# Four of six gate chunks of the last batch by Strassen's scheme, with sums formed a batch or two ahead

## The chip, the cores and the metric

The kernel runs on one core of a Trainium2 chip (trn2). The metric is device time in microseconds (us) from one launch, lower is better. The core has TensorE (PE: matrix products into the eight banks of PSUM), VectorE (DVE), ScalarE (ACT) and GpSimd (POOL) for element-wise work, and SyncE (SP), whose queue issues nearly all DMA transfers of this kernel. Each engine works through its own list of instructions in order and waits on semaphores for the others.

## The reference

```python
# q, k, v: 4 batches x 8 heads x 576 tokens x 64; everything float32
attn = softmax(q @ k.T / 8 + min(bias, 0), causal)      # bias from a running sum of max(s, 0)
x = concat_heads(attn @ v)                              # 2304 x 512
x = (silu(x @ w_gate) * (x @ w_val)) @ w_out            # 512 -> 1536 -> 512, "layer 1"
x = silu(x @ w_in2) @ w_out2                            # 512 -> 2048 -> 512, "layer 2"
```

## The kernel before

Every float32 product is made of three: each operand is split into a rounded high part and a low rest, and `mm3` issues high x high, high x low and low x high into one PSUM bank. Layer 1 runs batch by batch (0 to 3), each batch in nine chunks (`L1`): six "gv" chunks (gate and value columns for 256 of the 1536 hidden units) and three "o1" chunks (product with `w_out`). I number the chunks through: 0 to 35, batch 3 is 27 to 35. A gv chunk has four steps (`gate`: 2 groups of 128 hidden units x 2 halves of 288 tokens); a step has 24 matmuls of 128 x 128 by 128 x 288 for the gate, in one bank, and for the value, in a second, so a chunk has 96. ACT applies Silu (batch 3; Tanh before) to the gate's bank, DVE multiplies it with the value's bank (L534), ACT rounds the product to `h` high (L112), GpSimd subtracts for `h` low (L536). The pool `ps_m` has four banks, so the step after next takes the banks again: gate bank free after Silu, value bank free after L534. In batches 0 to 2 attention for the next batch is woven between the steps.

Weights of a chunk come as two 1 MB halves from DRAM (`w_half`, L396), where batch 0 has put them split into high and low; the pool has room for two chunks, so a chunk's load is issued when the chunk before the previous one is done. Beside layer 1 runs the preparation of layer 2's weights: raw pieces are loaded (`ahead_load`), decoded by ACT and DVE (`ahead`, L409 to L415), summed by GpSimd (`u_sum`, L473), cut by ACT and GpSimd (`u_cut`, L481) and stored (`u_store`, L486). Layer 2 already uses Strassen's scheme (`up2`, `down2`): seven products of sums of quarter blocks in place of eight.

What sets the order: PE's order is written by hand everywhere. Until the end of batch 2 a scheduler orders the other engines; in batch 3 and after all engines work in the order of the code.

Of the kernel before, what the change touches and what calls it, by code (L numbers as in the profile page):

```python
# [66 lines left out]
def kernel(  # L67
# [751 lines left out]
    def body():  # L819
# [101 lines left out]
        g = nc.gpsimd
        for c in range(last, n1):
            cur = chunk_steps(c)
            k = c - last
            more = [[] for _ in range(4)]
            extra = []
            if c + 1 < n1:
                more[0] += [lambda e=e: w_half(c + 1, e) for e in range(2)]
            i = tail_pieces.get(c)
            if i is not None:  # L930
                more[1].append(lambda i=i: ahead(i))
                if i % 2:
                    more[1].append(lambda q=i // 2: u_sum(q))
                    for e in range(2):
# [133 lines left out]
```

## Time and profile before

| what | value |
|---|---|
| device time of three runs | 1004.8, 1007.87, 1009.32 us; median 1007.87 us |
| the profiled execution's own time | 1005.74 us |
| its span, first to last instruction | 1004.0 us |
| PE, DVE, ACT, GpSimd busy | 99%, 56%, 52%, 59% of the span |
| granted TensorE clock | 1.00 after the first fortieth of the span |
| first and last matmul of batch 3 start at | 531.17 and 646.07 us |

The spans below are of the profiled execution. A busy share says how long an engine had any instruction in flight; whether it bounds the kernel is read from who waited for whom.

### The profile page before, as it was taken

The numbers are of one execution on the slowest core, as the hardware profiler recorded it, in microseconds if no ns is written. First come the engines' busy times: TensorE is split into PE (matmuls) and PEld (weight loads), VectorE is DVE, ScalarE is ACT, GpSimd is POOL, SyncE is SP. The second block draws the span as 40 slices with busy tenths as digits, with TensorE's granted clock in tenths as the row PEclk, the third lists the DMA queues.
The fourth block names the chain that finished last, engine by engine and source line by source line (L and its number), as shares of the span: only waits on it lengthen the run. The fifth ranks groups of instructions, "written<-read, shape, count | busy, mean of one in ns | idle before, by whom it ended". The sixth has DMA issues, their size and how long they took to land.

```text
span 1004.0 us, 19497 instructions
## 1 busy us (share of the span) xinstructions
PE 990.0 (99%) x6924; PEld 929.5 (93%) x6924; DVE 557.9 (56%) x1408; ACT 522.8 (52%) x1267; POOL 592.6 (59%) x748
## 2 busy tenths in 40 slices
PE   8999999999999999999999999999999999999998
PEld 6588889999998899899899999999999999999998
DVE  6868576635546544535542323366666667665555
ACT  6779788525666435656533543244544335543333
POOL 5967747515876555747541665356567458674445
PEclk8999999999999999999999999999999999999999
DMA  8898779667788799766768776797867866896662
GB/s 222 213 329 301 263 272 307 216 222 247 279 295 273 254 309 307 278 235 234 261 242 298 268 293 249 271 379 285 293 238 279 320 219 247 298 342 234 246 224 101
DMA packets 81618, 267.17 MB, mean 266 GB/s; under 512 B 9904, under 2 KB 29360, under 8 KB 66160
## 3 DMA queue, kind: packets, MB, share of 16 engines
q1 hardware_dynamic: 81376, 265.73, 75.7%
q8 instruction: 54, 0.88, 0.3%
q14 instruction: 44, 0.36, 0.1%
q10 hardware_dynamic: 144, 0.20, 0.1%
HBM read 208.15 MB, written 57.75 MB: 265 GB/s over the span
## 4 chain that ended last, share of the span: by engine, by line
PE 89%; ACT 4%; DMA 3%; DVE 2%; issue 1%; POOL 1%; SPq 0%; POOLq 0%; DVEq 0%; ACTq 0%
PE pgv L522 9%; PE pgv L523 9%; PE pgv L524 9%; PE po L709 6%; PE po L710 6%; PE po L711 6%; PE pu L664 6%; PE pu L667 6%; PE pu L668 6%; PE po L522 5%; PE po L523 5%; PE po L524 5%; PE pv L351 5%; PE psc L218 4%; PE ptr L302 3%; ACT e L255 2%
## 5 line engine op out<-in xcount | busy, mean ns | idle before, releaser
L522 PE MATMUL pgv<-xt,wt 128*128 128x288 f32 x768 | 229.7, 299 | 2.1 <-DVE u L533 1.7
L523 PE MATMUL pgv<-xt,wt 128*128 128x288 f32 x768 | 226.2, 294 | 0.0
L524 PE MATMUL pgv<-xt,wt 128*128 128x288 f32 x768 | 226.1, 294 | 0.0
L641 POOL TENSOR_TENSOR h<-u,h 128x384 fp32r<-128x384 f32 x72 | 75.1, 1044 | 142.5 <-ACT h L112 134.9
L522 PEld LDWEIGHTS pgv<-xt,wt 128*128 128x128 f32 x768 | 144.1, 188 | 13.7 <-DVE m L235 6.3
L523 PEld LDWEIGHTS pgv<-xt,wt 128*128 128x128 f32 x768 | 144.1, 188 | 0.0
L524 PEld LDWEIGHTS pgv<-xt,wt 128*128 128x128 f32 x768 | 144.0, 188 | 0.0
L536 POOL TENSOR_TENSOR h<-u,h 128x288 fp32r<-128x288 f32 x96 | 78.9, 824 | 87.3 <-ACT h L112 85.0
L112 ACT ACTIVATE h<-u 128x288 fp32r<-128x288 f32 (+1 forms) x168 | 79.8, 475 | 97.0 <-DVE u L534 95.9
L522 PE MATMUL po<-h,wt 128*128 128x288 f32 x384 | 114.8, 299 | 0.0
L523 PE MATMUL po<-h,wt 128*128 128x288 f32 x384 | 113.1, 294 | 0.0
L524 PE MATMUL po<-h,wt 128*128 128x288 f32 x384 | 113.0, 294 | 0.0
L709 PE MATMUL po<-h,wt 128*128 128x384 f32 x336 | 112.4, 335 | 0.0
L710 PE MATMUL po<-h,wt 128*128 128x384 f32 x336 | 112.3, 334 | 0.0
L711 PE MATMUL po<-h,wt 128*128 128x384 f32 x336 | 112.3, 334 | 0.0
L664 PE MATMUL pu<-x,wt 128*128 128x384 f32 x330 | 111.8, 339 | 0.3 <-DMA wt<-wu_d 0.3
L668 PE MATMUL pu<-x,wt 128*128 128x384 f32 x330 | 111.7, 339 | 0.0
L667 PE MATMUL pu<-x,wt 128*128 128x384 f32 x330 | 111.7, 339 | 0.0
L641 POOL TENSOR_TENSOR h<-t,h 128x384 fp32r<-128x384 f32 x96 | 106.7, 1133 | 5.5 <-ACT h L112 5.5
L255 ACT ACTIVATE e<-e,m 64x64 f32<-64x64 f32 (+4 forms) x160 | 88.2, 553 | 30.7 <-DVE m L235 29.9
L670 ACT ACTIVATE s<-pu 128x384 f32<-128x384 f32 x48 | 23.6, 492 | 150.2 <-PE pu L668 150.2
L720 DVE TENSOR_TENSOR acc<-po,acc 128x384 f32<-128x384 f32 x144 | 76.8, 558 | 36.3 <-PE po L711 35.6
(115 smaller groups left out, 2187.4 us busy)
## 6 DMA issues: line engine op xcount, KB each, us to landing
wt<-w_d SPq DMA_DIRECT2D x54, 1024.0 KB, 7.0
wt<-wu_d SPq DMA_DIRECT2D x48, 1024.0 KB, 9.2
wt<-wu_d SPq DMA_DIRECT2D x47, 768.0 KB, 6.6
r<-in_w_dram SPq DMA_DIRECT2D x36, 512.0 KB, 6.5
w_d<-wt SPq DMA_DIRECT2D x18, 1024.0 KB, 8.4
r<-in_w_dram SPq DMA_DIRECT2D x64, 256.0 KB, 7.3
qkr<-in_qk_dram SPq DMA_DIRECT2D x32, 288.0 KB, 9.0
cumb<-cum_d SPq DMA_DIRECT2D x15, 576.0 KB, 9.7
```

The costliest lines, as they stand in the source:

```text
L112: act_last[:] = [nc.scalar.activation(out=out, in_=in_, func=AF.Copy, scale=scale).ins]
L255: nc.scalar.activation(out=e[:r, hd, :wd], in_=e[:r, hd, :wd], func=AF.Exp, bias=m[hd][:r], scale=-1.0, accum_out=put[hd],)
L522: nc.tensor.matmul(out=ps[:, :n], lhsT=a, rhs=xh, start=(k == 0), stop=False)
L523: nc.tensor.matmul(out=ps[:, :n], lhsT=a, rhs=xl, start=False, stop=False)
L524: nc.tensor.matmul(out=ps[:, :n], lhsT=c, rhs=xh, start=False, stop=(k == last))
L641: nc.gpsimd.tensor_tensor(out=h[:, 1], in0=u, in1=h[:, 0].bitcast(F32), op=ALU.subtract)
L664: nc.tensor.matmul(out=o, lhsT=a, rhs=x[:, 0, kk], start=fresh and kk == 0, stop=False, skip_group_check=True)
L667: nc.tensor.matmul(out=o, lhsT=a, rhs=x[:, 1, kk], stop=False, **more)
L668: nc.tensor.matmul(out=o, lhsT=c, rhs=x[:, 0, kk], stop=kk == 1, **more)
L709: nc.tensor.matmul(out=ps, lhsT=a, rhs=h[:, 0], start=fresh, stop=False, skip_group_check=True)
L710: nc.tensor.matmul(out=ps, lhsT=a, rhs=h[:, 1], stop=False, **more)
L711: nc.tensor.matmul(out=ps, lhsT=c, rhs=h[:, 0], stop=e == 1, **more)
```

## The change

In batch 3 the gv chunks at places 1, 2, 4 and 5 of the nine (chunks 28, 29, 31 and 32) use Strassen's scheme on 2 x 2 blocks (input halves x token halves). `quad` computes the gate (e = 0) and then the value (e = 1), each in seven products of six matmuls of 288 columns: 42 for each, 84 in a chunk. The four quarter results of the gate lie in the four banks of `ps_m`, those of the value in four banks of `ps_o`. Adding up the products takes, for each e, two ACT copies (`s0`, `s1`) and four DVE additions (`w`, and three more), of which two (into bank c and from it into `s1`) stand between the fourth product and the seventh, which adds to bank c.

Four sums of weight blocks for each of these chunks are formed by DVE from the split weights while these are in SBUF for batch 1 (gate half) and batch 2 (value half) (`s_make`, one addition 512 wide and four 128 wide, 16 times), stored to DRAM (16 transfers of 256 KB) and loaded again in batch 3 (`z_load`, 8 of 512 KB), where ACT rounds (`s_high`) and DVE subtracts (`s_low`, 1024 wide, both inputs in SBUF). The sums of the tokens are formed by DVE in two halves, the first in chunk 26, the second at the start of chunk 27 (`t_sum`, `t_cut`). The side work of batch 3 gets new places (a table of steps); `x2_load` moves from chunk 27 to chunk 30. Tanh writes straight into `u`, and the pool for `u` has three buffers in place of two.

```diff
+QUAD = (1, 2, 4, 5)
+MAKE = {
+    (1, 1): (2, 3), (1, 2): (0, 3), (1, 4): (1, 3), (1, 5): (0, 3),
+    (2, 1): (0, 2), (2, 2): (1, 3), (2, 4): (0, 2), (2, 5): (1, 3),
+}
...
-            th = tmp.tile([P, HB], F32, tag="th", name="th")[:, :n]
-            nc.scalar.activation(out=th, in_=pg[:, :n], func=AF.Tanh, scale=0.5)
+            nc.scalar.activation(out=u, in_=pg[:, :n], func=AF.Tanh, scale=0.5)
...
+    def t_sum(i, kk):
...
+            v.tensor_tensor(out=t, in0=a[:, 0], in1=b[:, 0], op=ALU.subtract)
+            v.tensor_tensor(out=d, in0=a[:, 1], in1=b[:, 1], op=ALU.subtract)
+            v.tensor_tensor(out=t, in0=t, in1=d, op=ALU.add)
+            return
...
+        v.tensor_tensor(out=t, in0=a[:, 0], in1=t, op=ALU.subtract)
+        v.tensor_tensor(out=t, in0=t, in1=a[:, 1], op=ALU.add)
+
+    def t_cut(i, kk, eng):
...
+        copy("a", x[:, 0], t)
+        eng.tensor_tensor(out=x[:, 1], in0=t, in1=x[:, 0].bitcast(F32), op=ALU.subtract)
+
+    def s_make(c, e, kk):
...
+        nc.vector.tensor_tensor(out=zs, in0=hi, in1=lo, op=ALU.add)
...
+            nc.vector.tensor_tensor(out=o, in0=a, in1=b, op=op)
+        nc.sync.dma_start(out=z_d[QUAD.index(place[stream[c]]), e, kk], in_=z)
...
+    def s_high(k, e):
+        qd["s", k, e] = qd["sp"].tile([P, 2, CW // 2], F32R, tag="sq", name="sq")
+        copy("a", qd["s", k, e][:, 0], qd["z", k, e])
+
+    def s_low(k, e):
+        s = qd["s", k, e]
+        nc.vector.tensor_tensor(out=s[:, 1], in0=qd["z", k, e], in1=s[:, 0].bitcast(F32), op=ALU.subtract)
+
+    def quad(c, i, e, pos):
...
+        if xi in (0, 1):
+            nc.scalar.activation(out=part(f"s{xi}"), in_=o, func=AF.Copy)
+        if xi == 3:
+            v.tensor_tensor(out=part("w"), in0=o, in1=qd["s0"], op=ALU.add)
+        if xi in (4, 5):
+            v.tensor_tensor(out=o, in0=o, in1=qd["w"], op=ALU.add)
+        if xi == 4:
+            v.tensor_tensor(out=qd["s1"], in0=o, in1=qd["s1"], op=ALU.add)
+            close(3, qd["s1"])
+        if xi in (2, 5, 6):
+            close({2: 0, 5: 1, 6: 2}[xi], o)
...
+        for i, at in ((1, -1), (4, -1), (3, -1), (6, 0)):
+            at_step(0, at, t_sum, i, 1)
+            at_step(0, at, t_cut, i, 1, v)
```

On DVE, at the start of chunk 27, this stood before (u is the product with the value's bank, dk and z32 decode a piece for layer 2):

```order
L565 SCALAR_TENSOR_TENSOR acc3_6384<-po_7679,acc3_6384 128x288
L534 TENSOR_TENSOR u_7742<-pgv_7729,u_7742 128x288
L534 TENSOR_TENSOR u_7777<-pgv_7764,u_7777 128x288
L412 SCALAR_TENSOR_TENSOR dk_7783<-z32_7782,dk_7783 128x512
L415 SCALAR_TENSOR_TENSOR z32_7782<-r64_7646,dk_7783 128x512
L534 TENSOR_TENSOR u_7818<-pgv_7805,u_7818 128x288
L534 TENSOR_TENSOR u_7853<-pgv_7840,u_7853 128x288
```

And this stands there now, from chunk 27's second gate product to the first additions of chunk 28 (tq and xq: token sums; sq: weight sums, zq as loaded; pq: banks of the scheme):

```order
L606 TENSOR_TENSOR xq_7611<-tq_7795,xq_7611 128x288
L540 TENSOR_TENSOR u_7879<-pgv_7866,u_7879 128x288
L633 TENSOR_TENSOR sq_7884<-zq_7791,sq_7884 128x1024
L540 TENSOR_TENSOR u_7916<-pgv_7903,u_7916 128x288
L633 TENSOR_TENSOR sq_7921<-zq_7793,sq_7921 128x1024
L419 SCALAR_TENSOR_TENSOR dk_7927<-z32_7926,dk_7927 128x512
L422 SCALAR_TENSOR_TENSOR z32_7926<-r64_7713,dk_7927 128x512
L540 TENSOR_TENSOR u_7961<-pgv_7948,u_7961 128x288
L683 TENSOR_TENSOR w_7990<-pq_7983,s0_7975 128x288
L633 TENSOR_TENSOR sq_7981<-zq_7887,sq_7981 128x1024
L685 TENSOR_TENSOR pq_8007<-pq_8007,w_7990 128x288
L687 TENSOR_TENSOR s1_8002<-pq_8007,s1_8002 128x288
```

Two weight sums and the decode now stand before the fourth product, and a third weight sum before the additions into bank c. Ahead of these rows, between acc3 and the second product, DVE has eight more rows of token sums.

On ACT, in the same stretch (u: Silu; h: high part; xq and sq: high parts of the sums), before:

```order
L529 ACTIVATE u_7742<-pgv_7716 128x288
L112 ACTIVATE h_7715<-u_7742 128x288
L529 ACTIVATE u_7777<-pgv_7751 128x288
L112 ACTIVATE h_7715<-u_7777 128x288
L409 ACTIVATE z32_7782<-r64_7646 128x512
L410 ACTIVATE dk_7783<-r64_7646 128x512
L529 ACTIVATE u_7818<-pgv_7792 128x288
L112 ACTIVATE h_7791<-u_7818 128x288
L529 ACTIVATE u_7853<-pgv_7827 128x288
```

And now, from the second Silu on:

```order
L536 ACTIVATE u_7879<-pgv_7853 128x288
L118 ACTIVATE h_7813<-u_7879 128x288
L118 ACTIVATE sq_7884<-zq_7791 128x1024
L536 ACTIVATE u_7916<-pgv_7890 128x288
L118 ACTIVATE h_7889<-u_7916 128x288
L118 ACTIVATE sq_7921<-zq_7793 128x1024
L416 ACTIVATE z32_7926<-r64_7713 128x512
L417 ACTIVATE dk_7927<-r64_7713 128x512
L536 ACTIVATE u_7961<-pgv_7935 128x288
L118 ACTIVATE h_7889<-u_7961 128x288
L681 ACTIVATE s0_7975<-pq_7968 128x288
L118 ACTIVATE sq_7981<-zq_7887 128x1024
```

The fourth Silu stands behind two weight sums and the decode, and the first copy of chunk 28 (`s0`) behind that.

On DVE, in chunk 21 (batch 2), ten rows of `s_make` (zm, two sums at once, for chunk 22) now stand around the last minimum of the scores (L242, two rows, L235 before) and ahead of the reciprocal that followed right behind it. The first six of the twelve rows there:

```order
L614 TENSOR_TENSOR zm_6633<-wt_6279 128x512
L614 TENSOR_TENSOR zm_6739<-wt_6279 128x512
L242 ISA e_6288,m_6332<-psc_6296,e_6288,m_6330 128x64
L242 ISA m_6332 128x1
L620 TENSOR_TENSOR zm_6633<-zm_6633 128x128
L620 TENSOR_TENSOR zm_6739<-zm_6739 128x128
```

The minimum, the reciprocal and what follows them now come after one pair of 512-wide additions, and the reciprocal after eight 128-wide ones too.

## Rows read from the trace of the kernel before

**Rows 1.** The page: busy time of the engines; the chain that ended last.
```profile
PE 990.0 (99%) x6924; PEld 929.5 (93%) x6924; DVE 557.9 (56%) x1408; ACT 522.8 (52%) x1267; POOL 592.6 (59%) x748
...
PE 89%; ACT 4%; DMA 3%; DVE 2%; issue 1%; POOL 1%; SPq 0%; POOLq 0%; DVEq 0%; ACTq 0%
```
**Rows 2.** Windows of batches 1, 2, 3: stretch, length, busy us by engine, clock, DMA.
```profile
220.65:375.87 155.22, 155.22 (x1206) 141.68 (x1205) 80.53 (x253) 86.74 (x233) 98.78 (x148) 1.00 0.82 280
375.87:531.17 155.30, 154.17 (x1195) 140.93 (x1193) 75.72 (x247) 86.24 (x232) 90.26 (x137) 1.00 0.74 255
531.17:646.40 115.23, 114.90 (x868) 114.70 (x867) 33.19 (x60) 44.67 (x88) 61.57 (x55) 1.00 0.76 279
```
**Rows 3.** Timeline of PE: first matmul of chunks 27 and 28, last of batch 3.
```profile
531.17 0.29 PE L522 MATMUL pgv<-xt,wt 128*128 128x288 f32 x1
...
543.89 0.29 PE L522 MATMUL pgv<-xt,wt 128*128 128x288 f32 x1
...
646.07 0.30 PE L524 MATMUL po<-h,wt 128*128 128x288 f32 x1
```
**Rows 4.** Timelines of PE and SP at batch 3's one gap (chunk 32).
```profile
596.22 0.29 PE L524 MATMUL pgv<-xt,wt 128*128 128x288 f32 x1
596.84 0.37 PE L522 MATMUL pgv<-xt,wt 128*128 128x288 f32 x1 [0.33 <-DMA wt<-w_d]
...
586.93 0.93 SPq L396 DMA_DIRECT2D wt<-w_d  x2
```
**Rows 5.** ACT and DVE in batch 3, by form: busy us, mean ns, idle before.
```profile
L112 ACT ACTIVATE h<-u 128x288 fp32r<-128x288 f32 x24 | 10.7, 445 | 34.6 <-DVE u L534 34.6
L529 ACT ACTIVATE u<-pgv 128x288 f32<-128x288 f32 x24 | 9.6, 402 | 17.1 <-PE pgv L524 14.5 <-POOL h L536 2.6
L112 ACT ACTIVATE cut<-s 128x1024 fp32r<-128x1024 f32 x4 | 4.2, 1044 | 0.0
...
L534 DVE TENSOR_TENSOR u<-pgv,u 128x288 f32<-128x288 f32 x24 | 10.9, 456 | 49.5 <-PE pgv L524 43.6 <-ACT u L529 4.1 <-POOL x L597 1.7
```
**Rows 6.** DVE with both inputs in SBUF, alone and beside GpSimd.
```profile
L618 DVE TENSOR_TENSOR stage<-x2r 128x384 f32<-128x384 f32 x4 | 2.2, 548 | 0.0
...
599.14 0.95 DVE L618 TENSOR_TENSOR tt<-x2r,tt 128x768 f32<-128x768 f32 x1
...
560.41 1.83 DVE L618 TENSOR_TENSOR tt<-x2r,tt 128x768 f32<-128x768 f32 x1
...
559.58 1.85 POOL L597 TENSOR_TENSOR x<-x2r,x 128x768 fp32r<-128x768 f32 x1
```
**Rows 7.** Timeline of DVE at chunk 27: last addition of chunk 26, fourth product.
```profile
531.37 0.46 DVE L565 SCALAR_TENSOR_TENSOR acc<-po,acc 128x288 f32<-128x288 f32 x1 [1.14 <-PE po L524]
...
544.16 0.46 DVE L534 TENSOR_TENSOR u<-pgv,u 128x288 f32<-128x288 f32 x1 [2.44 <-PE pgv L524]
```
**Rows 8.** Timeline of ACT in chunk 27: table, first Silu, decode, fourth Silu.
```profile
532.99 1.28 ACT L529 ACT_TABLE_LOAD   x1 [4.63 <-PE pgv L524]
534.28 0.41 ACT L529 ACTIVATE u<-pgv 128x288 f32<-128x288 f32 x1
...
538.67 0.66 ACT L409 ACTIVATE z<-r 128x512 f32<-128x512 f32 x1
...
542.55 0.41 ACT L529 ACTIVATE u<-pgv 128x288 f32<-128x288 f32 x1 [0.35 <-PE pgv L524]
```
**Rows 9.** DMA of `w_half` in batch 3, 16 issues.
```profile
DMA to landing us min/median/max: 5.4/7.6/10.0
```
**Rows 10.** Timeline of DVE in chunk 21: idle before its last wait.
```profile
442.76 0.22 DVE L235 CUSTOM_DVE_ANT_0 e<-psc,e 64x64 f32<-64x64 f32 x1 [6.78 <-PE psc L218]
```
**Rows 11.** Timelines of ACT and PE at the two gaps of batch 2.
```profile
400.02 1.06 ACT L112 ACTIVATE cut<-s 128x1024 fp32r<-128x1024 f32 x1 [3.99 <-DMA wu_d<-cut]
...
401.98 0.40 PE L522 MATMUL pgv<-xt,wt 128*128 128x288 f32 x1 [0.40 <-DVE u L533]
...
414.01 0.49 PE L351 MATMUL pv<-pt,vz 128*64 128x320 f32 x2 [0.74 <-DVE u L533]
```

More of the change, by code (lines that the diff above doesn't have):

```diff
@@ L92 @@
     dec_p = pool("dec", 2, scope=first_layer)
-    tmp_p = pool("tmp", 2, scope=first_layer)
+    tmp_p = pool("tmp", 3, scope=first_layer)
     h_p = pool("h", 6, scope=first_layer)
@@ L125 @@
     x2_d = dram.tile([KD, P, NT], F32, name="x2_d")
+    z_d = dram.tile([len(QUAD), 2, 2, P, DW], F32, name="z_d")
     w64 = w.bitcast(U32).rearrange("c p (n t) -> c p n t", t=2)
@@ L575, in chunk_steps @@
         kind, i = stream[c]
+        if batch[c] == B - 1 and place[stream[c]] in QUAD:
+            return [lambda e=e, n=n: quad(c, i, e, n) for e in range(2) for n in range(len(UP))]
         if c == 0:
@@ L911, in body @@
                 stp()
+                if n in MAKE.get((b, c % len(L1)), ()):
+                    s_make(c, b - 1, MAKE[b, c % len(L1)].index(n))
+                if c == last - 1 and n == 1:
+                    for i in (1, 3, 4, 6):
+                        t_sum(i, 0)
+                        t_cut(i, 0, nc.gpsimd)
             for p in at[4]:
@@ L916, in body @@
         everything.enter_context(tc.manual_schedule(engines=None))
-        p2["x2"] = pool("x2", 10, scope=second_layer, side="right")
         p2["x2r"] = pool("x2r", 2, scope=second_layer, side="right")
         p2["ps"] = pool("ps_o", 4, PS, scope=second_layer, side="right")
-        stores = []
-        g = nc.gpsimd
+        quads = ExitStack()
+        for name, n in (("sp", 4), ("zp", 2), ("tmp", 2), ("sum", 1)):
+            qd[name] = pool("q" + name, n, scope=quads, side="right")
+        plan = {}
@@ new lines, in body @@
+        for k in range(NCH - NPR - 1):
+            for e in range(2):
+                at_step(k, 0, w_half, last + k + 1, e)
+        for x, e, at, load in (
+            (1, 0, (0, 1), (2, 0)), (1, 1, (0, 2), (2, 1)), (2, 0, (1, 0), (4, 0)), (2, 1, (1, 7), (4, 1)),
+            (4, 0, (2, 0), (5, 0)), (4, 1, (2, 7), (5, 1)), (5, 0, (3, 0), None), (5, 1, (3, 2), None),
+        ):
+            k, n = at
+            at_step(k, n, s_high, x, e)
+            n += k in QUAD
+            at_step(k, n, s_low, x, e)
+            if load:
+                at_step(k, n, z_load, *load)
@@ L922, in body @@
+        at_step(7, 3, u_load, 1, "Z")
+        at_step(8, 0, u_load, 0, "ZS")
         for c in range(last, n1):
-            cur = chunk_steps(c)
             k = c - last
[L925 to L934, printed above, removed]
-                        more[2 + e].append(lambda q=i // 2, k=e: u_cut(q, k))
-                        more[2 + e].append(
-                            lambda q=i // 2, k=e: stores.extend(lambda e=e: u_store(q, k, e) for e in range(2))
-                        )
@@ L954, in body @@
[L954 to L958 removed]
+            for n, stp in enumerate([None] + chunk_steps(c), -1):
                 if n == 0:
                     wst.pop(c - 1, None)
[L961 to L967 removed]
@@ L968, in body @@
-        for f in stores:
-            f()
+                if stp is not None:
+                    stp()
+                for f in plan.get((k, n), []):
+                    f()
         first_layer.close()
```

156 lines of the change are left out of this document (121 added, 35 removed).

## The prediction

> **What bounds the kernel now.** The page comes first: PE has something in flight 99% of the span, no other engine over 59%, and the chain that ended last runs 89% on PE [rows 1]. A busy share alone would not prove a bound, so the windows are next: in batches 1 and 2 PE idles 0 and 1.1 us of 155, and in batch 3 0.3 of 115, while DVE is busy 80.5, 75.7 and 33.2 us [rows 2]. Batch 3 runs from 531.17 to 646.07 us. Its first chunk takes 543.89 - 531.17 = 12.72 us for 96 matmuls, 0.1325 us each [rows 3]; a matmul's own 0.29 us is the length of the pipeline, not its price. The single gap is in chunk 32: the next matmul starts 0.62 us after its predecessor instead of 0.13, so 0.49 us are lost to a weight half that was issued late (586.93, where other halves go out when the chunk before starts) [rows 4]. So a matmul that goes away is worth its 0.1325 us, as long as nothing makes PE wait.
>
> **What is removed.** Four chunks go from 96 to 84 matmuls of the same width: 48 x 0.1325 = 6.36 us. In the new order the weight halves of chunk 32 stand behind loads and stores that are ready by then, so I count the gap of 0.49 us as gone too. Together 6.85 us.
>
> **What it costs in chunks 27 to 29.** Prices first. ACT: a 288-wide copy or rounding 0.45, Silu 0.40, a 1024-wide rounding 1.04 us. DVE with one input in PSUM: 0.46 us [rows 5]. Two SBUF inputs alone: 384 wide 0.55 and 768 wide 0.95, so 1.04 ns a column, 288 wide 0.45 and 1024 wide 1.21 us [rows 6]. Back-to-back instructions overlap by 0.1 us, a dependent one starts 0.05 to 0.1 us late.
>
> Now the queues. The token sums of chunk 27 can't be finished before DVE has taken the last result of chunk 26, at 531.37 to 531.83, as it did before [rows 7]. From there it is a chain between DVE and ACT: last addition of the second sum (532.2), ACT's rounding (532.7), DVE's rest (533.2), the third sum's two operations (534.1), rounding (534.6), and only then the activation table of 1.28 us, which before ran from 532.99, and the first Silu, which before started at 534.28 [rows 8]. I get Silu done at 536.2 and its product at 536.7, 1.5 us later than before. The fourth sum (to 538.7), the second Silu (538.4) and h (539.5) follow, then the weight sum's rounding (to 540.5), the third Silu (540.8), h (542.6), the second weight sum (543.6), two decodes like the 0.66 us one (to 544.7), and the fourth Silu, done at 545.0 instead of 542.96 [rows 8]. On DVE the rest of the second weight sum and the decode (two operations 512 wide, 0.68 us each) end at 546.2, so the fourth product ends at 546.6, where before it ran from 544.16 to 544.62 [rows 7].
>
> PE begins chunk 28 at 543.89 and wants the fourth product's bank for its fourth result at 543.89 + 18 x 0.1325 = 546.28: it gets it at 546.65, a wait of 0.4 us. ACT comes to the first copy (s0) at 547.0, then rounds a weight sum for chunk 29 (to 548.3), then copies s1 (548.6): bank d, wanted at 548.2, is 0.4 us late. DVE waits with that sum's rest for the rounding and ends it at 549.6; the two additions behind it end at 550.5, and the seventh result wants bank c at 549.45: 1.1 us. So 1.9 us in the first half of chunk 28.
>
> In its second half and in the first of chunk 29 a weight sum's rest again stands just ahead of the two additions. Undisturbed, these would start when the fourth result is done, 3.35 us into a half, and end at 4.4, ahead of the 4.77 us at which the seventh starts. With the 1.21 us operation started after the rounding, some 2.5 us in, they end at 4.8 to 5.3. I take 0.45 us for the one, with GpSimd's u_sum beside it, and 0.85 us for the other, where ACT also has four h of the chunk before to round first. The second half of chunk 29 just fits, and chunks 31 and 32 have no weight sum in them: 4.4 against 4.77 us, no wait. Sum 3.2 us; from below it is 0 (if DVE's part starts earlier than I read it), from above 3.2 and what GpSimd adds (third rival).
>
> **DMA.** The 8 loads of z are 4.2 MB on top of 279 GB/s [rows 2]. Each is issued when DVE has emptied its buffer, some 5 us ahead of use. A 1 MB half lands in 5.4 to 10.0 us [rows 9], and half the bytes should take nearer the low end: no wait. The halves themselves stay one chunk (11.1 us) ahead; at most their late end, 10.0 us, would show.
>
> **What it costs in batches 1 and 2.** The 16 weight sums are 16 x (0.68 + 4 x 0.28) = 29 us of DVE by the line of [rows 6], in 310 us where DVE idles 154 [rows 2]. The scheduler put them where DVE was idle: the cluster in chunk 21 (3.6 us) lies ahead of an idle stretch of 6.78 us [rows 10]. What it can't hide: GpSimd's locks stretch them, and 16 more stores stand in SP's queue. How a late store costs is seen in batch 2: ACT sat 3.99 us waiting for a store to land, the Tanh behind it came late, DVE's L533 too, and PE idled 0.40 us; the other gap is 0.74 us [rows 11]. I take one more such gap, 0.5 us, of 0 to 16. The first half of the token sums (10 operations) falls into chunk 26, where DVE has only the additions: 0, with some 0.5 us of room at the sixth result there.
>
> **Sum.** 1005.74 - 6.85 + 3.2 + 0.5 = 1002.6 us for an execution like the profiled one. The median of the runs shown, 1007.87, is 2.1 us above that execution, so I predict 1004.7 us. Of three equal runs the spread was 4.5 us; 0.5%, about 5 us, is what a measurement tells from no change.
>
> **The rivals.**
>
> *All hidden.* The 6.85 us arrive whole: 1001.0 us. For it: DVE and ACT are busy only 33 and 45 of 115 us in batch 3 [rows 2]. Against it: the share says nothing on the place; the waits above come from 15 us in which ACT and DVE wait for each other in turn.
>
> *GpSimd holds DVE up.* An operation of DVE with two SBUF inputs took 1.83 us where it takes 0.95 alone; GpSimd's ran until 561.43, DVE's began at 560.41 and ended 0.81 us after that [rows 6]. If each of the four weight sums in chunks 28 and 29 meets such an operation, each costs 0.88 us more; 0.6 us of that is in my sum already, so 4 x 0.88 - 0.6 = 2.9: 1007.6 us, no change. Against it: in the order of the changed kernel GpSimd has mostly 288-wide operations there, and gaps. The Trainium skill (SBUF — State Buffer, Who interferes with whom) says that DVE with two SBUF inputs and a reading GpSimd take one shared port by an exclusive lock, and the second "fully blocks". By that rule each of the four would wait for all that is left of GpSimd's operation, as in this rival; the trace agrees, with 0.81 us between the end of the one and of the other.
>
> *The weight sums of batches 1 and 2 hold PE up.* Price: a gap like the 0.74 us one [rows 11] for each of the 16, 11.8 us in place of 0.5: 1004.7 + 11.3 = 1016 us, slower. For it: DVE is half busy there and GpSimd busier (98.8 us of 155), so each 128-wide addition may wait longer than it runs. Against it: a bank is wanted only a step (some 4 us) after its product. It makes the kernel slower by over 0.5% only when 12 of the 16 cost that much.
>
> That the change doesn't do what it says is excluded: PE's list is 48 matmuls shorter.
>
> **How the numbers follow.** The likeliest is the sum as it stands (0.45; its own range 1002.5 to 1007). All hidden 0.25, GpSimd 0.2, batches 1 and 2 0.1. Faster by over 0.5% (below 1002.8) is the second case alone, 0.25; slower the last, 0.1; between them 0.65. From 1000 to 1010 us I leave out the last case and another tenth of misreadings.
>
> **What would show it.** In the changed profile, batch 3's PE should have 816 matmuls at the same 0.13 us, begin at about 531 and end some 3.6 us earlier than 646.07. Right: PE's waits in batch 3 name DVE (the fourth product, the additions into bank c) and ACT's copies, nearly all in chunks 28 and 29, some 3 us in all; chunks 31 and 32 take 11.1 us; the gap at chunk 32 is gone. Wrong: chunk 28 in 11.2 us means that the chain starts earlier than I read; a wait for wt or zq means that DMA is the price; a start of batch 3 off by over 1 us means that batches 1 and 2 paid or gained; 1.5 to 2.4 us for L633 means GpSimd.

## The result, and the profile after

The changed kernel takes 1019.97 us (median of four runs, 1018.45 to 1021.78), the kernel before 1007.62 us (four runs): a ratio of 1.0132, 95% interval 1.0114 to 1.0150. It is slower by 1.3%, where I forecast no change.

The profiled execution (own time 1019.63 us, span 1017.8) is 13.9 us longer than that of before. By the first matmuls of chunks 9 and 27 (531.17 in [rows 3], 540.12 now) and of layer 2:

| stretch | before | after | forecast of the difference | measured |
|---|---|---|---|---|
| start and batch 0 | 220.65 | 219.41 | 0 | -1.2 |
| batches 1 and 2 | 310.52 | 320.71 | +0.5 | +10.2 |
| batch 3 | 115.04 | 114.53 | -3.65 | -0.5 |
| layer 2 | 357.76 | 363.19 | 0 | +5.4 |

The page of the kernel after, busy time and the chain that ended last, against [rows 1]: PE has 48 matmuls less, as the diff says; the chain runs 74% on PE where it ran 89%, and 7% on DVE and 4% on GpSimd where it was 2% and 1%.

```profile
PE 990.8 (97%) x6876; PEld 927.2 (91%) x6876; DVE 641.6 (63%) x1556; ACT 538.2 (53%) x1299; POOL 603.9 (59%) x748
...
PE 74%; DVE 7%; ACT 5%; DMA 5%; POOL 4%; issue 4%; SPq 0%; POOLq 0%; DVEq 0%; ACTq 0%
```

Windows of the kernel after, batches 1, 2 and 3, against [rows 2] (stretch, length, busy us by engine, clock, DMA share, GB/s), and two short stretches:

```profile
219.41:381.65 162.24, 157.46 (x1206) 142.62 (x1205) 101.73 (x293) 86.42 (x233) 102.15 (x148) 0.99 0.83 281
381.65:540.12 158.47, 154.56 (x1195) 140.94 (x1194) 100.52 (x303) 87.74 (x237) 97.95 (x141) 1.00 0.77 270
540.12:654.65 114.53, 110.73 (x819) 108.61 (x818) 71.09 (x113) 58.61 (x115) 62.03 (x51) 1.00 0.81 296
...
259.40:262.70 3.30, 3.26 (x16) 1.96 (x17) 1.34 (x4) 2.25 (x7) 3.30 (x8) 0.50 0.86 350
...
665.60:672.40 6.80, 5.33 (x17) 5.36 (x18) 1.02 (x2) 0.90 (x2) 1.72 (x3) 0.50 1.03 417
```

PE idles 4.8 and 3.9 us in batches 1 and 2 (0 and 1.1 before) and 3.8 us in batch 3. DVE has 21 and 25 us more. The last two rows are stretches at a granted clock of 0.50 (1.2 GHz, half of full speed).

Timeline of PE in the kernel after: the largest gap of batch 1 (chunk 11), one of batch 2 (chunk 21), the first of chunk 28, the first of chunk 34, and the first of layer 2. [In brackets]: idle time before, and who ended it. A gap is counted here from the start of one matmul to the start of the next, so the usual step of 0.13 us (0.18 in layer 2) is in it.

```profile
256.44 0.29 PE L531 MATMUL pgv<-xt,wt 128*128 128x288 f32 x1
259.44 0.80 PE L358 MATMUL pv<-pt,vz 128*64 128x320 f32 x2 [2.71 <-DVE u L539]
...
443.98 0.30 PE L323 MATMUL ptr<-ident,z 128*128 128x128 f32 x1 [1.65 <-DVE m L242]
...
558.15 0.29 PE L664 MATMUL pq<-xt,sq 128*128 128x288 f32 x1
559.28 0.40 PE L660 MATMUL pq<-xq,wt 128*128 128x288 f32 x1 [0.84 <-DVE s L687]
...
629.81 0.40 PE L529 MATMUL pgv<-xt,wt 128*128 128x288 f32 x1 [0.50 <-ACT u L536]
...
662.93 0.34 PE L793 MATMUL pu<-x,z 128*128 128x384 f32 x1
667.07 0.66 PE L789 MATMUL pu<-x,wt 128*128 128x384 f32 x1 [3.80 <-DMA wt<-wu_d]
667.52 0.52 PE L792 MATMUL pu<-x,wt 128*128 128x384 f32 x1
```

The gap of chunk 11 is longer than both gaps of [rows 11] together; the one of layer 2 costs again after it, since the matmuls behind it run at half the clock (0.32 us apart in place of 0.18). In batch 3 six gaps of 0.7 to 1.1 us stand: three in chunks 28 and 29, ended by DVE's addition (L687), one in chunk 31, ended by an ACT copy (L569), and two in chunk 34, ended by ACT's Silu (L536) and by DVE's addition (L571). The gap of [rows 4] is gone.

Timeline of DVE in the kernel after, at those places: chunk 10 ahead of the gap of chunk 11, chunk 21, chunk 28, chunk 34.

```profile
245.28 0.68 DVE L614 TENSOR_TENSOR zm<-wt 128x512 f32<-128x512 f32 x1
247.38 1.05 DVE L614 TENSOR_TENSOR zm<-wt 128x512 f32<-128x512 f32 x1 [1.43 <-DMA z_d<-zm]
248.36 0.44 DVE L539 SCALAR_TENSOR_TENSOR u<-u,pgv 128x288 f32<-128x288 f32 x1
248.73 1.25 DVE L620 TENSOR_TENSOR zm<-zm 128x128 f32<-128x128 f32 x2
249.90 0.45 DVE L540 TENSOR_TENSOR u<-pgv,u 128x288 f32<-128x288 f32 x1
250.27 2.62 DVE L620 TENSOR_TENSOR zm<-zm 128x128 f32<-128x128 f32 x6
252.81 0.44 DVE L539 SCALAR_TENSOR_TENSOR u<-u,pgv 128x288 f32<-128x288 f32 x1
...
442.31 1.32 DVE L614 TENSOR_TENSOR zm<-wt 128x512 f32<-128x512 f32 x2 [3.05 <-DMA wt<-w_d]
443.55 0.27 DVE L242 CUSTOM_DVE_ANT_0 e<-psc,e,m 128x64 f32<-128x64 f32 x1
...
451.73 0.22 DVE L242 CUSTOM_DVE_ANT_0 e<-psc,e 64x64 f32<-64x64 f32 x1 [5.47 <-PE psc L225]
...
557.06 1.23 DVE L633 TENSOR_TENSOR sq<-zq,sq 128x1024 fp32r<-128x1024 f32 x1 [0.49 <-ACT sq L118]
558.21 0.46 DVE L685 TENSOR_TENSOR pq<-pq,w 128x288 f32<-128x288 f32 x1
...
628.97 2.69 DVE L422 SCALAR_TENSOR_TENSOR z<-r,dk 128x512 uint32<-128x512 uint32 x1
```

Three things are to be seen. In chunk 10 the second 512-wide addition waits 1.43 us for a store of an earlier sum to land, since the two buffers are shared with the decode; L539 and L540, which PE needs, stand behind it and between the narrow additions, which take up to 2.62 us for six. In chunk 21 the sums of chunk 22 wait 3.05 us for chunk 22's weights, and the minimum (L242), which the attention of the next batch needs, stands behind them: it starts at 443.55, and the transposes of PE at 443.98. The idle stretch of [rows 10] is still there behind all this, 5.47 us long, and unused. In chunk 28 a weight sum's rest stands right ahead of the additions, as I had read it.

ACT passes the delay of chunk 10 on. Timeline of ACT in the kernel after (chunk 11: a cut and the Tanh behind it; then chunk 30's decode and the copies behind it):

```profile
256.38 1.04 ACT L118 ACTIVATE cut<-s 128x1024 fp32r<-128x1024 f32 x1
...
258.44 0.39 ACT L538 ACTIVATE u<-pgv 128x288 f32<-128x288 f32 x1
...
590.84 0.67 ACT L416 ACTIVATE z<-r 128x512 f32<-128x512 f32 x1 [3.39 <-DMA r<-in_w_dram]
591.41 0.65 ACT L417 ACTIVATE dk<-r 128x512 uint32<-128x512 uint32 x1
591.96 0.69 ACT L569 ACTIVATE acc<-po 128x288 f32<-128x288 f32 x2
```

Behind the narrow additions stand DVE's minima (from 253.73, 4.2 us into chunk 11; before 0.4 us ahead of it), for which ACT's exponentials wait, and behind these the cut and the Tanh. The Tanh runs 8.9 us into the chunk, before 4.7 (255.51 - 250.78); DVE's L539 waits for it and PE for L539, and 2.9 of these 4.2 us arrive at PE.

DVE in the kernel after by form (busy us, mean ns, idle before), batches 1 and 2, then batch 3:

```profile
L620 DVE TENSOR_TENSOR zm<-zm 128x128 f32<-128x128 f32 x64 | 28.7, 471 | 0.4
...
L614 DVE TENSOR_TENSOR zm<-wt 128x512 f32<-128x512 f32 x16 | 12.7, 796 | 4.5 <-DMA wt<-w_d 3.1 <-DMA z_d<-zm 1.4
...
L633 DVE TENSOR_TENSOR sq<-zq,sq 128x1024 fp32r<-128x1024 f32 x8 | 11.4, 1427 | 5.7 <-ACT sq L118 5.5
```

SP's queue ahead of layer 2: the last store of the prepared weights in the kernel before, then the start of layer 2 in the kernel after (wu_d: layer 2's weights; x_d: layer 2's input):

```profile
639.57 0.32 SPq L486 DMA_DIRECT2D wu_d<-s  x1
```

```profile
652.20 0.41 SPq L493 DMA_DIRECT2D wu_d<-cut  x1
655.27 0.32 SPq L493 DMA_DIRECT2D wu_d<-s  x1
655.74 2.76 SPq L573 DMA_DIRECT2D x_d<-acc  x3
658.58 5.93 SPq L756 DMA_DIRECT2D wt<-wu_d  x7
```

The last stores of the prepared weights (q = 15) went out at 632.43 to 639.57 before, 14 to 7 us ahead of layer 2; now they go out from 649.48 to 655.27, and layer 2 begins at 654.65. The load for which PE waits follows at 658.58, 3.9 us into layer 2 (3.0 before), and PE goes on 8.5 us after that (5.9 before).

### The profile page after: what moved, and what is told of

It is laid out like the page before. It is cut to its first block, busy times and chain, and to the rows that moved or that the text cites. A ratio compares the mean times of both kernels' runs of the same rounds, so it can differ in the third digit from the quotient of the medians.

```text
span 1017.8 us, 19629 instructions
## 1 busy us (share of the span) xinstructions
PE 990.8 (97%) x6876; PEld 927.2 (91%) x6876; DVE 641.6 (63%) x1556; ACT 538.2 (53%) x1299; POOL 603.9 (59%) x748
## 4 chain that ended last, share of the span: by engine, by line
PE 74%; DVE 7%; ACT 5%; DMA 5%; POOL 4%; issue 4%; SPq 0%; POOLq 0%; DVEq 0%; ACTq 0%
PE pu L789 6%; PE po L835 6%; PE po L834 6%; PE po L836 6%; PE pu L793 6%; PE pu L792 6%; PE pgv L529 5%; PE pgv L530 5%; PE pgv L531 5%; PE po L529 4%; PE pv L358 4%; PE po L530 4%; PE po L531 4%; PE ptr L309 3%; PE psc L225 2%
## 5 line engine op out<-in xcount | busy, mean ns | idle before, releaser
L529 PE MATMUL pgv<-xt,wt 128*128 128x288 f32 x640 | 192.2, 300 | 2.1 <-DVE u L539 1.1
L530 PE MATMUL pgv<-xt,wt 128*128 128x288 f32 x640 | 188.4, 294 | 0.0
L531 PE MATMUL pgv<-xt,wt 128*128 128x288 f32 x640 | 188.4, 294 | 0.0
L529 PEld LDWEIGHTS pgv<-xt,wt 128*128 128x128 f32 x640 | 120.0, 188 | 14.3 <-DVE m L242 3.6
L530 PEld LDWEIGHTS pgv<-xt,wt 128*128 128x128 f32 x640 | 120.1, 188 | 0.0
L531 PEld LDWEIGHTS pgv<-xt,wt 128*128 128x128 f32 x640 | 120.0, 188 | 0.0
L529 PE MATMUL po<-h,wt 128*128 128x288 f32 x384 | 115.0, 299 | 0.0
L542 POOL TENSOR_TENSOR h<-u,h 128x288 fp32r<-128x288 f32 x80 | 66.6, 837 | 58.0 <-ACT h L118 58.0
## 6 DMA issues: line engine op xcount, KB each, us to landing
cumb<-cum_d SPq DMA_DIRECT2D x15, 576.0 KB, 10.2
```

The source lines that it names most:

```text
L529: nc.tensor.matmul(out=ps[:, :n], lhsT=a, rhs=xh, start=(k == 0), stop=False)
L530: nc.tensor.matmul(out=ps[:, :n], lhsT=a, rhs=xl, start=False, stop=False)
L531: nc.tensor.matmul(out=ps[:, :n], lhsT=c, rhs=xh, start=False, stop=(k == last))
```

## The experiments

All times by the same sections as above; median, and ratio against the kernel before on the same chip (its median there was 1005.7 to 1007.1 us for e1 to e16). Profiles of kernels with the same code in batches 1 and 2 (after, e5 to e8, e11, e13) gave 318.4 to 322.9 us for these, so a single difference under some 4.5 us between two of them says little; the four without DVE's sums (e1, e2, e9, e14) gave 309.0 to 310.6. The stretch up to chunk 9 varied from 219.4 to 224.5 us.

| kernel | batches 1, 2 | batch 3 | layer 2 | median us | ratio, 95% interval |
|---|---|---|---|---|---|
| before | 310.5 | 115.0 | 357.8 | 1007.6 | |
| after | 320.7 | 114.5 | 363.2 | 1020.0 | 1.0132 (1.0114 to 1.0150) |
| e1 no sums | 309.0 | 115.3 | 362.0 | 1008.0 | 1.0027 (1.0012 to 1.0041) |
| e2 stores only | 310.6 | 114.6 | 362.1 | 1008.8 | 1.0024 (1.0010 to 1.0038) |
| e3 sums unstored | 315.6 | 116.1 | 363.0 | 1017.6 | 1.0120 (1.0100 to 1.0139) |
| e4 before, with sums | 322.6 | 114.5 | 356.8 | 1017.0 | 1.0120 (1.0092 to 1.0147) |
| e5 rests later | 318.4 | 116.6 | 361.9 | 1022.2 | 1.0161 (1.0137 to 1.0184) |
| e6 no last stores | 322.9 | 115.7 | 356.7 | 1017.5 | 1.0112 (1.0089 to 1.0135) |
| e7 load first | 320.6 | 115.5 | 361.1 | 1019.5 | 1.0134 (1.0110 to 1.0159) |
| e8 decode in PSUM | 319.2 | 115.6 | 361.6 | 1018.1 | 1.0112 (1.0079 to 1.0146) |
| e9 mended, no sums | 309.7 | 121.4 | 361.5 | 1016.8 | 1.0095 (1.0075 to 1.0114) |
| e10 two chunks | 314.2 | 115.4 | 358.1 | 1011.9 | 1.0055 (1.0033 to 1.0077) |
| e11 mended | 321.0 | 119.5 | 358.4 | 1024.6 | 1.0172 (1.0152 to 1.0193) |
| e12 sums in batch 0 | 316.2 | 119.8 | 358.1 | 1020.6 | 1.0127 (1.0095 to 1.0159) |
| e13 light mending | 319.0 | 115.9 | 356.8 | 1013.6 | 1.0085 (1.0060 to 1.0109) |
| e14 light, no sums | 309.3 | 114.7 | 356.8 | 1006.3 | 0.9990 (0.9974 to 1.0006) |
| e15 one input | 321.6 | 114.0 | 361.1 | 1017.2 | 1.0114 (1.0085 to 1.0143) |
| e16 half width | 318.3 | 114.7 | 360.1 | 1018.2 | 1.0105 (1.0085 to 1.0124) |

**What batches 1 and 2 pay for.** Theory A: DVE's additions, in front of work that PE waits for. Theory B: the stores. Theory C: the small edits. Four kernels take the parts away one by one.

e1, without sums and stores:

```diff
-                if n in MAKE.get((b, c % len(L1)), ()):
-                    s_make(c, b - 1, MAKE[b, c % len(L1)].index(n))
...
-in_=z_d[QUAD.index(k), e].rearrange("k p n -> p k n")
+in_=w1_d[k, e][:, :, :DW]
```

> The changed kernel without the 16 weight sums of batches 1 and 2: neither DVE's additions nor the stores; batch 3 loads the same bytes from the split weights instead, so its products are of other numbers. Theory A (DVE's additions, standing in DVE's queue in front of work that PE waits for, cost the 10.2 us by which batches 1 and 2 grew) and theory B (the 16 stores cost them: SP's queue, and buffers that wait for a store to land) both expect batches 1 and 2 to take 310 to 311 us again, in place of 320.7, and the whole about 10 us less than the changed kernel, near 1010 us. Theory C (the small edits cost them: Tanh into u, three buffers) expects no difference, 1019 to 1021 us. Layer 2's first gap of 4.1 us stays in all of them.

e2, stores only:

```diff
-        z = dec_p.tile([P, DW], U32, tag="dk", name="zm").bitcast(F32)
...
-        nc.sync.dma_start(out=z_d[QUAD.index(place[stream[c]]), e, kk], in_=z)
+        hi = wst[c][e][0].bitcast(F32)
+        nc.sync.dma_start(out=z_d[QUAD.index(place[stream[c]]), e, kk], in_=hi[:, kk * DW : kk * DW + DW])
```

> The changed kernel with the 16 stores of batches 1 and 2 in place, but from the split weights as they are: DVE's 80 additions are left out. Theory A (the additions cost the 10.2 us) expects it within 1.5 us of the run without sums, near 1010 us. Theory B (the stores) expects most of the loss to be back, 1017 to 1020 us.

e3, additions without stores:

```diff
-        nc.sync.dma_start(out=z_d[QUAD.index(place[stream[c]]), e, kk], in_=z)
...
-in_=z_d[QUAD.index(k), e].rearrange("k p n -> p k n")
+in_=w1_d[k, e][:, :, :DW]
```

> The changed kernel with DVE's 80 additions in batches 1 and 2, but without the 16 stores: batch 3 loads the same bytes from the split weights. Theory A expects most of the loss to remain, 1017 to 1020 us. Theory B expects it to go, 1010 to 1012 us. Where both matter (the wait of the second 512-wide addition for a store to land was 1.4 us of the 3 us gap in chunk 11), it is about halfway, 1014 us.

e4, the kernel before with the sums:

```diff
                 stp()
+                if n in MAKE.get((b, c % len(L1)), ()):
+                    s_make(c, b - 1, MAKE[b, c % len(L1)].index(n))
```

> The kernel before with the 16 weight sums and their stores added in batches 1 and 2, and nothing else: what is stored is not used, batch 3 is as before. Theories A and B expect 7 to 11 us more than the kernel before, 1015 to 1019 us, with the gaps of PE in batches 1 and 2 naming DVE. Theory C expects 1007 to 1010 us.

Windows of batches 1 and 2 in e1, then in e4:

```profile
219.78:374.97 155.19, 155.19 (x1207) 141.70 (x1205) 80.56 (x253) 86.79 (x233) 98.78 (x148) 1.00 0.82 279
374.97:528.78 153.81, 153.81 (x1195) 140.93 (x1194) 84.40 (x263) 88.21 (x237) 94.58 (x141) 1.00 0.75 264
```

```profile
221.04:384.48 163.44, 157.23 (x1207) 143.21 (x1205) 102.05 (x293) 86.04 (x233) 102.03 (x148) 0.99 0.82 278
384.48:543.68 159.20, 156.16 (x1195) 141.77 (x1194) 92.33 (x287) 86.01 (x232) 93.09 (x137) 0.99 0.76 262
```

Without the sums PE is busy in every microsecond of both batches; with them alone, batches 1 and 2 lose 12.1 us. Theory C falls: with the small edits and no sums, batches 1 and 2 take 1.5 us less than before, and batch 0 took 159.7 to 160.4 us in the kernels that have these edits and no sums there, against 161.4 and 161.5 in before and e4. So the small edits gained a little, and against e1 the sums cost 11.7 us. The stores alone cost 0.1 us against before and 1.6 against e1 (e2), so theory B falls as the main cause. Theory A stands: e3, without stores, is 9.6 us slower than e1, which has the same batch 3 and layer 2, by the medians, 6.6 of them in batches 1 and 2 of the profiled executions. By the same medians the changed kernel is 10.7 us slower than e1 (each against before on its chip). How much the stores add to the additions stays open. The wait for a store in chunk 10 was not what made the gap behind it: in e3, which stores no sum, five narrow additions there took 3.56 us, and the gap in chunk 11 is again 3.0 us. Timeline of PE in e3:

```profile
260.14 0.49 PE L358 MATMUL pv<-pt,vz 128*64 128x320 f32 x2 [2.71 <-DVE u L539]
```

Is it the additions' own time, or GpSimd's conflict with them? A weight sum's 128-wide additions took 281 ns where GpSimd was idle (16 of the 64) and 534 ns on average beside it (48). e15 gives them one SBUF input each, e16 half the columns:

```diff
-        nc.vector.tensor_tensor(out=zs, in0=hi, in1=lo, op=ALU.add)
+        v.tensor_reduce(out=z.rearrange("p (a n) -> p a n", a=2), in_=pair, op=ALU.add, axis=X)
...
+            v.tensor_reduce(out=z[:, o * P : o * P + P], in_=pair[:, a, f * P : f * P + P], op=ALU.add, axis=X)
```

> The changed kernel with the five operations of each weight sum in a form with one SBUF input: they read pairs of high and low part and add them (so the sums lack the differences, and batch 3's products are of other numbers), with the same columns written. Alone these should take about 1.1 us and 0.4 us in place of 0.68 and 0.28, so that DVE's time for them is some 43 us, as the two-input sums took beside GpSimd. If the cost is the time that stands in DVE's queue, the loss stays within 3 us of the changed kernel's, 1017 to 1022 us. If it is the conflict with GpSimd on both sides, no operation is lengthened and half of the loss or more goes, 1010 to 1014 us.

```diff
+        v.tensor_tensor(out=z[:, : 4 * h], in0=hi[:, : 4 * h], in1=lo[:, : 4 * h], op=ALU.add)
+        a11, a21, a12, a22 = [z[:, k * h : k * h + h] for k in range(4)]
...
-        nc.sync.dma_start(out=z_d[QUAD.index(place[stream[c]]), e, kk], in_=z)
```

> The changed kernel with weight sums of half the width (256 and 64 columns), stored not at all; batch 3 loads the split weights instead. Compared with the run with sums unstored (batches 1 and 2 took 315.6 us, 5.0 us more than before). If the cost follows the columns that DVE adds, it halves: 312.5 to 313.5 us. If it follows the number of operations in the queue and their waits, it stays at 315 us or more.

Of these operations of e15, the line's summary (min, median, max ns), and in the kernel after the same for L620:

```profile
L615 DVE TENSOR_REDUCE zm<-wt x64: 400/416/432, 245.9 to 483.1; 128x128 f32<-128x256 f32 x64
```

```profile
L620 DVE TENSOR_TENSOR zm<-zm x64: 275/292/1846, 240.3 to 479.0; 128x128 f32<-128x128 f32 x64
```

With one SBUF input no operation is stretched, and the loss stays all the same: 11.1 us for 46.5 us of DVE (10.2 for 42.9 after). So the loss doesn't need the conflict, which is one way in which the time in the queue grew; what 29 us without any stretching would have cost, no run shows. e16 halves the columns, but its 64-wide additions took 412 ns on average (203 at least), so DVE's time fell only to 34.2 us from e3's 42.4. Batches 1 and 2 lost 7.8 us (5.0 in e3), and the time is as far above before as in e3, 11.2 us by the medians: fewer columns brought nothing. That the place of an addition in the queue is what counts is read from the waits above and not shown by a run of its own: the order of DVE was made anew in each of these kernels, so they can't be told apart more finely.

**Batch 3: the place of the rests.**

```diff
-            n += k in QUAD
+            n += 5 * (k in QUAD)
             at_step(k, n, s_low, x, e)
             if load:
                 at_step(k, n, z_load, *load)
```

> The changed kernel with the four rests of weight sums (L633) of the Strassen chunks four products later: behind the sixth product of a half instead of behind the second, so that they no longer stand ahead of the additions into bank c. If their place is what holds PE up (as in the prediction), the three gaps of 1.13, 0.82 and 1.13 us in chunks 28 and 29 go, batch 3 takes 111.5 to 112 us in place of 114.5, and the time is some 2.7 us less than the changed kernel, near 1017 us. If ACT's copies set the end anyway (the other theory), chunks 28 and 29 keep 13.7 and 12.3 us.

Chunk 28 fell from 13.74 to 12.08 us, so the place was 1.7 of the 2.6 us that it lost. But chunks 29 and 30 rose to 13.76 and 14.53 (12.29 and 12.71 after), and the time did not fall. Timelines of DVE, of SP and of PE in e5:

```profile
566.91 2.46 DVE L633 TENSOR_TENSOR sq<-zq,sq 128x1024 fp32r<-128x1024 f32 x1
573.29 2.98 DVE L633 TENSOR_TENSOR sq<-zq,sq 128x1024 fp32r<-128x1024 f32 x1
```

```profile
569.43 0.38 SPq L625 DMA_DIRECT2D zq<-z_d  x1
...
570.89 2.02 SPq L403 DMA_DIRECT2D wt<-w_d  x2
```

```profile
582.40 0.40 PE L529 MATMUL po<-h,wt 128*128 128x288 f32 x1 [1.44 <-DMA wt<-w_d]
```

The later rests met GpSimd (2.46 and 2.98 us). The load of the next sum waits for the rest's buffer, which came free at 569.37, and held up SP's queue: chunk 30's weights went out at 570.89, 4.8 us into chunk 29 (1.9 after), and PE lost 0.8 and 1.6 us to their two halves. A waiting transfer is a place in a queue too.

**Layer 2's first gap.** e6 leaves the last piece's stores out, e7 moves the load:

```diff
-            for i in range(2):
+            for i in range(2 if q < 15 else 0):
                 at_step(*put, u_store, q, e, i)
```

> The changed kernel without the four stores of the last pieces (q = 15), which stand in SP's queue at the end of chunk 35; the last step of layer 2 loads the pieces of the step before instead, so its products are of other numbers. If these stores, late since their piece is summed and cut late, delay the load for which PE waits 4.1 us in layer 2, the gap falls to 0.7 us or less, the half clock behind it goes, and the time is about 5 us less, near 1015 us. If the load is late for another reason (its buffer, or the stores of the sums of chunk 35), the gap stays at 3 us or more.

```diff
         at_step(8, 0, u_load, 0, "ZS")
+        at_step(8, 5, u_load, 1, "S")
...
-        u_load(1, "S")
```

> The changed kernel with one load moved: that of the second step's S weights, for which PE waits in layer 2, stands two stores earlier in SP's queue, still behind the stores of the last pieces. If it is only SP's order, it is issued 1.5 to 2.9 us sooner and the gap falls from 4.1 to 1.5 to 2.5 us. If it is the traffic of the late stores that slows the load (8.5 us to land in place of 5.9), the gap stays above 3 us.

In e6 the gap is gone altogether and layer 2 takes 356.7 us, 6.5 less than after. In e7 the gap is 2.85 us in place of 4.13: SP's order is a third of it; the rest goes with the late stores themselves, in the queue or as traffic.

**The side work of chunks 30 to 34.** e8 decodes three pieces through PSUM:

```diff
+            if i in (27, 30, 31):
+                wst["dk", i] = p2["ps"].tile([P, 512], F32, tag="o", name="dk").bitcast(U32)
```

> The changed kernel with the decoding of three pieces (in chunks 30, 33 and 34) through a bank of PSUM, as before, in place of SBUF: DVE's decode then has one input in PSUM. In chunk 34 this decode took 1.77 and 2.69 us beside GpSimd, in place of 0.69. If GpSimd's hold on DVE's operations with two SBUF inputs costs the gaps of 0.79 and 0.70 us there, chunk 34 takes 12.7 to 13.2 us in place of 14.16 and the last piece is stored earlier too, so the time is 1 to 3 us less. If ACT's order of side work costs them, chunk 34 stays at 14 us.

Chunk 34 took 13.49 us in place of 14.15: the gap that DVE's addition ended is gone, the one that ACT's Silu ended is left. So the conflict was about half of it. The whole is no nearer to before (12.4 us above it, as the changed kernel).

**Mending, and smaller changes.** e9, e11 and e12 put the four remedies together (with the edits of e7 and e8):

```diff
-            n += k in QUAD
+            n += 5 * (k in QUAD)
...
-                at_step(k, n, z_load, *load)
+                at_step(*((k + 1, 0) if k in QUAD and e else (k, n)), z_load, *load)
...
-(27, (3, 4))
+(27, (3, 7))
...
-(15, 1, (8, 0), (8, 4))
+(15, 1, (8, 0), (8, 6))
```

> The run without weight sums (its products of the sums are of other numbers), with batch 3 mended at four places: the rests of weight sums behind the sixth product, with the loads of the second halves moved behind the weights of the next chunk, since they held these up in the run with later rests; the decoding of three pieces in PSUM; the piece of chunk 30 decoded behind that chunk's copies and not ahead of them; layer 2's load issued ahead of the stores of the last piece's second part. If the missing 6 us of batch 3 and the 5 us of layer 2 are these four and nothing else, batch 3 takes 109 to 111 us (115.0 before), layer 2 begins without a gap above 1 us, and the time is 7 to 10 us less than the run without sums, 998 to 1001 us, 0.6% to 1% below the kernel before. If the waits only move to the next thing that is late, as in the run with later rests, it is 1005 us or more.

> The changed kernel with its weight sums as they are, and batch 3 mended at the same four places. If batches 1 and 2 and the rest are separate costs, it is 10 us above the mended run without sums and 7 to 10 us below the changed kernel, 1009 to 1013 us, still slower than before. If the mending only moves waits, 1017 us or more.

e12 besides moves four sums:

```diff
-    (1, 1): (2, 3), (1, 2): (0, 3), (1, 4): (1, 3), (1, 5): (0, 3),
+    (0, 1): (2, 3), (1, 2): (0, 3), (0, 4): (1, 3), (1, 5): (0, 3),
```

> The same mended kernel with four of the sixteen weight sums (those of the gate halves of chunks 1 and 4 of a batch) formed in batch 0 in place of batch 1, where PE's gaps of 3.0 us with the half clock behind it and of 2.0 us followed them. If DVE is free for them in batch 0, batch 1 loses nothing and batch 0 little: 5 to 7 us below the mended kernel with all sums in batches 1 and 2. If batch 0's DVE, which also decodes layer 1's weights, is late by them too, PE's gaps only move to batch 0 and it is within 3 us of the other, or above.

All three lost: chunk 29 took 17.0 to 19.2 us. Timeline of ACT in e9:

```profile
565.73 0.41 ACT L684 ACTIVATE s<-pq 128x288 f32<-128x288 f32 x1 [0.44 <-PE pq L667]
572.07 1.06 ACT L118 ACTIVATE sq<-zq 128x1024 fp32r<-128x1024 f32 x1 [5.92 <-DMA zq<-w_d]
```

The load that I had moved behind the weights came too late, and ACT waited 5.92 us for it with the copy that PE needed next behind it. Chunk 31 took 11.2 us in all three (12.09 after), so chunk 30's decode was its cost. With four sums in batch 0 (e12) batches 1 and 2 took 316.2 us, 4.8 less than in e11, and batch 0 162.0, 1.9 more; by the medians it is 4.0 us faster.

e10 has the scheme in two chunks only:

```diff
-QUAD = (1, 2, 4, 5)
+QUAD = (2, 5)
```

> A smaller change, as a candidate: only chunks 2 and 5 of the last batch by Strassen's scheme, with the eight weight sums (of the places at which no gap of PE followed), and the mending of batch 3 as far as it applies. It saves 24 matmuls, 3.2 us, and the gap of 0.5 us. If the sums at these places are hidden and batch 3 has no new wait, 1002 to 1004 us, 0.3% below the kernel before. If the sums cost as much each as the others did (0.64 us), 1007 to 1009 us.

Eight sums at the places that had looked free cost 3.7 us in batches 1 and 2 (5.2 against e1, which has no gap there): a place that had no gap behind it was not a free one. Batch 3 took 115.4 us, 0.4 more than before, so the 24 matmuls fewer brought nothing either.

e13 and e14 are lighter:

```diff
-            n += k in QUAD
+            n += (5 if (x, e) == (2, 0) else 1) * (k in QUAD)
...
-((7, 2), "c", 5), ((7, 3), "c", 6)
+((8, 0), "c", 5), ((8, 1), "c", 6)
...
-(15, 0, (7, 3), (8, 2)), (15, 1, (8, 0), (8, 4))
+(15, 0, (7, 3), (8, 1)), (15, 1, (7, 3), (8, 2))
```

> The changed kernel with its weight sums, and a lighter mending: the decoding of three pieces in PSUM; chunk 30's piece decoded behind that chunk's copies; two cuts of layer 2's tokens behind the last piece's cuts, so that this piece is stored some 4 us sooner, and layer 2's load ahead of two stores; one rest of a weight sum (the first of chunk 28) behind the sixth product, the others as in the change. If the late last piece is what layer 2 waits for, its gap of 4.1 us falls under 1 us and layer 2 takes 357 to 359 us; if chunk 30's piece is what holds chunk 31 up, that takes 11.2 us. Together 6 to 8 us less than the changed kernel, 1012 to 1014 us. If the waits only move, 1018 us or more.

> The same lighter mending without the weight sums of batches 1 and 2 (its products of the sums are of other numbers). If batches 1 and 2 cost 10 us by the sums alone and the rest is mended, 1001 to 1003 us, which is what the change was worth in batch 3 alone. If not, 1006 us or more.

SP's queue at the start of layer 2 in e13 (which begins at 655.08):

```profile
651.89 0.55 SPq L496 DMA_DIRECT2D wu_d<-s  x1
652.52 2.21 SPq L576 DMA_DIRECT2D x_d<-acc  x3
655.01 0.61 SPq L759 DMA_DIRECT2D wt<-wu_d  x1
```

The last store goes out 3.2 us ahead of layer 2 and not 0.6 behind its start, the load with the start, and PE has no gap there: layer 2 takes 356.8 us, 6.4 less, and the whole is 6.4 us less than the changed kernel. Chunk 31 takes 11.20 us, but batch 3 as a whole 1.4 us more than after (chunks 33 and 35 14.34 and 14.14 us), so what was gained is layer 2. Without the sums (e14) the same kernel is even with before, 0.9990, not the 1001 to 1003 us I expected: chunks 28 and 29 still took 14.07 and 12.28 us, and a late weight half opened a gap of 1.1 us in chunk 35. No kernel that computes the sums was faster than before.

## Why the prediction was wrong

**The gain was sized right.** 48 matmuls are gone (6924 to 6876), the matmul's step is still 0.13 us, and the gap of [rows 4] is gone. But e4, whose batch 3 is that of before, has no such gap either, so that its 0.49 us are the change's is not shown.

**Chunks 28 and 29: the mechanism was right, the size nearly.** Forecast 3.2 us of waits, measured 2.61 + 1.16 = 3.77 (13.74 and 12.29 us against 84 matmuls, 11.13 us). The first half of chunk 28 lost 1.8 us where I had 1.9, its second half and the first of chunk 29 lost 0.8 and 1.1 where I had 0.45 and 0.85. PE waited 1.0 us at the seventh result of chunk 28, where I had 1.1, for the additions behind a weight sum's rest. GpSimd's rival came in part: two rests took 1.71 and 1.75 us in place of 1.23.

**Chunks 31 and 34: left out of the sum.** I had followed DVE's additions into chunk 31 and found them in time. It lost 0.96 us to ACT, which waited 3.39 us for a piece's load with chunk 30's copies behind it; e13 and e14 take that away. Chunk 34 lost 1.43 us in two gaps. The second was DVE's, whose addition stood behind decodes and cuts of layer 2's tokens, which the changed kernel crowds into chunks 33 and 34; e8 takes it away, 0.66 us. The first, ended by ACT's Silu, stands in every kernel with the changed batch 3, and its cause is open.

**Layer 2: not in the sum at all**, 5.4 us. I counted DMA in batch 3 by bytes and by the age of each load, but not what the later places of the side work do behind batch 3. The last stores are 5 to 9 us nearer to layer 2 than before; e6, which leaves them out, shows that they are the cause, and e13, which issues them sooner, agrees.

**Batches 1 and 2: the step that failed most.** "I take one more such gap, 0.5 us" measured 10.2 (11.7 against e1). Three readings were wrong. *The idle stretch.* I took DVE's idle 6.78 us in chunk 21 [rows 10] as room for the sums ahead of it. But work ahead of an idle stretch doesn't stand in it: the minimum and the reciprocal stand between. The weights landed at 442.31, DVE waited 3.05 us for them with the minimum behind, and PE lost 1.65 us, while the idle stretch, which began at 446.25, stayed empty. *The time.* 29 us alone became 42.9 beside GpSimd, which I had named and not priced. By the Trainium skill (SBUF — State Buffer, Who interferes with whom) a DVE operation with two SBUF inputs contends with a GpSimd one that reads SBUF, and `tensor_reduce` on trn2 does not; the traces agree, with 275 to 1846 ns for the one and 400 to 432 for the other. *The slack.* "A bank is wanted only a step after its product" is true of one wait, but in chunk 10 the delay went from DVE's minima to ACT's exponentials, cut and Tanh, and back to DVE and PE. The rival that I gave a tenth had the right place and nearly the sum (11.8 against 10.2 us), by another road: not sixteen gaps of 0.74 us, but five of 1 to 3 us and a stretch at half the clock. That its sum came so near is luck.

**Still open**: which of the sixteen sums could stand where without cost. Neither fewer columns, nor one input, nor batch 0, nor fewer chunks made them free. Whether they would be free inside DVE's idle stretches, behind the minima, no run tried.

## What to carry to other kernels

Idle time of an engine is room only for work that stands in it. Work that is put ahead of the idle time delays what stands between, all the more if it waits for its own input: look up when that input lands, and what stands behind the new work in the same queue. When side work is moved to make room for a scheme, follow it to its last store and to the first load that comes after, also past the end of the stretch that you change. A remedy that moves a wait moves whatever is queued behind it: moving the rests mended chunk 28 and cost chunks 29 and 30 more.

## What the runs showed of the hardware

In the kernel after, a PE gap of 3.0 us was followed by 3.41 us at half the clock (granted 0.50, from 259.38), and one of 4.1 us by 6.83 us (from 665.57), in which 17 matmuls stood 0.32 us apart in place of 0.18: some 2.4 us on top of the gap. It isn't certain: in e4 gaps of 2.96 and 2.47 us were followed by 3.41 us at half the clock, and one of 2.97 us wasn't.

On SP, the store issued at 655.27 in the kernel after had its data at 652.84, when GpSimd was done. Of SP's waits from 640 to 665 us this one names what held it for 2.4 us more:

```profile
SPq L493 <- DMA wt<-wu_d: 2.6, 1, 2.6
```

It waited for a load of layer 2's weights to land, at 655.21, that had gone out at 647.68, eight issues earlier. By the trace's issues and landings no transfer of SP's queue, of 514 here and 490 in the kernel before, was issued with more than seven older ones still on their way. So in this kernel a store can be held by a transfer that has nothing to do with it.
